# One attention-and-MLP kernel on one core: upper half-chains ten matmuls behind instead of fourteen, maxima eight steps ahead instead of seven, and transfers costed by kind in the order's planner

## The chip, the core and the metric

The kernel runs on one core of one Trainium2 chip. Its engines are TensorE (PE, with its weight loads shown apart as PEld), VectorE (DVE), ScalarE (ACT), GpSimd (POOL) and SyncE (SP), which here only issues transfers. The metric is the device time of one execution in microseconds (us).

## The reference, cut to what matters

Inputs are one sequence of 2048 rows of 512 numbers, four square weight matrices, two MLP weights of 512 x 1792 and 1792 x 512, and 32 gates, all float32.

```python
xn = layernorm(x)
q, k, v = xn @ wq, xn @ wk, xn @ wv            # 32 heads of 16, 4 segments of 512 rows
for s in range(4):
    logits = qs @ ks.T / 4 + mask              # mask adds -1e9 where key index > query index
    a_dot  = softmax(logits) @ vs
    a_mem  = phi(qs) @ M / (phi(qs) @ z + 1e-6)
    o      = g * a_mem + (1 - g) * a_dot
    M, z   = M + phi(ks).T @ vs, z + sum(phi(ks))
s = o @ wo
g = silu(relu(xn @ w1) @ w2)
out = x + s * g
```

`phi(t)` is `t + 1` for positive `t` and `exp(t)` otherwise. `M` and `z` are a memory carried from segment to segment.

## The kernel before, in words

The work is cut into four segments of 512 rows. A segment has four groups of eight heads, and a group (`n`, 0 to 15) two units of four heads (`u`, 0 to 31). For a unit the kernel computes the logits twice: once with queries on the partitions, only for the row maxima (`rowmax`, L1197 on PE, then the masked maximum L1203 on DVE), and once transposed (`expo`, L1249 on PE, then the exponential L1266 or L1260 on ACT). The maxima reach the second pass by a round trip: L1211 and L1212 on POOL, a transpose L1221 on DVE, a transfer to DRAM (L1223) and one back into a row of the stacked queries (L1224). `stack` (L1171) loads the queries and keys of a unit from DRAM into one of three slots. `pv` (L1295) multiplies the exponentials by the values.

Every large product is made of three matmuls for each float32 product (high part times high part, high times low, low times high). With a contraction of 128 rows it is split again into two halves of 64 rows, which lie in the lower and the upper half of the TensorE array and run side by side. A chain is all matmuls that add into one PSUM bank: twelve lower ones (L798) and twelve upper ones (L807), in the last part of the second MLP product six of each. By the code there are 176 such chains: 56 of the first MLP product, 64 of the second, 32 of the query and key projections, 12 of the value projection and 12 of the output projection. `lanes` writes them in pairs: each step gives PE one lower matmul and, taken from the queue `back`, one upper matmul of an earlier step. Upper and lower halves add into the same bank, so the first upper matmul of a chain waits on a semaphore, `turn`, which the last lower matmul of that chain increments (L801 to L807). A queue entry is taken when more than `BACK` entries lie in it, and a chain's first entry only when that chain's lower half has been written in full:

```python
if back and (len(back) > BACK or not m) and (not back[0][4] or back[0][1] in ended):
    high = back.popleft()
```

The order of all instructions on all engines is made before the kernel is built. Steps `t` run from -18 to 160; unit `v` has its five parts of `expo` in steps `5v` to `5v + 4`, and `rowmax` of unit `u` lies `LAG` steps earlier. Between these the chains are filled in. A planner (`Sched`) keeps a clock for each engine and one for the transfer rings, lets each engine take the pending operation with the earliest due time, and hands PE work by its own estimate of when operands are ready. `search` makes such an order several times, feeds back due times found backwards from what PE needed, and keeps the order with the earliest planned end. Nothing of the planner runs on the chip; only its order does.

Of the kernel before, what the change touches and what calls it, by code (L numbers as in the profile page):

```python
# [2 lines left out]

# [13 lines left out]
L = 512  # L17
D = 512
H = 32
# [17 lines left out]
FREE = 2  # L37
LAG = 7
BACK = 14
RESERVE = 20.48  # L40
# [3 lines left out]
PASSES = 12  # L44
FIRST = 3
FIT = 4
KEEP = False
SWITCH = 0.40
LOAD = 0.11
READ, WRITE = 1.0, 0.6  # L50
WARM = 1
# [31 lines left out]
class Sched:  # L83
# [175 lines left out]
def search(run, say=None):  # L259


    plan, total, ends, found = [], 560.0, {}, []
    for i in range(PASSES):
# [5 lines left out]
        if i < FIRST:  # L269
            continue  # L270
        e2 = ends
        for j in range(FIT):
            _, used, end, new, _ = run(plan, total, e2, taken)
            if say:
                say(i, j, end)
            assert [(str(a), b) for a, b in used] == [(str(a), b) for a, b in plan]
            found.append((end, plan, total, e2, taken))
            e2 = {k: 0.5 * v + 0.5 * e2.get(k, v) for k, v in new.items()}
        ends = min(found, key=lambda f: f[0])[3] if KEEP else e2
    return min(found, key=lambda f: f[0])  # L280


def emit(tc, PE, ACT, DVE, POOL, SP, cst, ps, dr, args, plan, left, ends, script=None):
# [155 lines left out]
    def planes():  # L439
        for nm, (t, k), c in (("q", DDR.next(), 0.0), ("k", DDR.next(), -1.0)):  # L440
            k = [f"{k}.{i}" for i in range(2)]
            pool(512, (), k, lambda t=t, c=c: POOL.memset(t, c), 0.0, 1e-3)
            for d, dk in SDR[nm].t:
                dma(k, [f"{dk}.c"], lambda d=d, t=t: SP.dma_start(d[:, 0, :], t), 2.0, 0.73, WRITE)

    def gates():
        dma((), ["bt"], lambda: SP.dma_start(bt, bass.AP(
            tensor=beta.tensor, offset=beta.offset, ap=[[0, 128], [1, H]])), 10.0, 0.1, 1.6)
        pool(10, (), ["pari"], lambda: POOL.iota(pari, pattern=[[0, 1]], base=0, channel_multiplier=1), 54.7)
# [30 lines left out]
    def load_one():  # L480
        nonlocal nload
        src, kn = plan[nload]
        raw, rk = IO.next(True)
        early = nload < 4
        dma((), [rk], lambda: SP.dma_start(raw.rearrange("p (k f) -> p k f", k=kn) if kn else raw, src),
            30.4 if early else 4.0, 0.93 if kn else 0.8)
        raws.append((raw, rk))
        nload += 1
# [103 lines left out]
    def lnload(s):  # L592
        LN[s] = xts = []
        for t in range(4):
            xt, k = IO.next(True)
            xts.append((xt, k))
            dma((), [k], lambda xt=xt, t=t: SP.dma_start(xt, x2[s * L + 128 * t:s * L + 128 * (t + 1), :]),
                7.2 if s == 0 else 8.0, 0.8)

# [281 lines left out]
    def silu(s, t):  # L881
# [9 lines left out]
        else:  # L891
            g, gk = gd[s]
            dma([k], [f"{gk}.{t}"], lambda: SP.dma_start(g[128 * t:128 * t + 128, :], sg), 18.7, 0.73, WRITE)
        if t == 3:
# [7 lines left out]
    def fetch(s, t):  # L902
# [5 lines left out]
        else:  # L908
            gt, gk = IO.next(True)
            g, k = gd[s]  # L910
            dma([f"{k}.{t}"], [gk], lambda: SP.dma_start(gt, g[128 * t:128 * t + 128, :]), 0.0, 0.85)
            xr, xk = IO.next(True)
        dma((), [xk], lambda: SP.dma_start(xr, x2[rows, :]), 11.2, 0.85)
        GX[s, t] = (gt, gk, xr, xk, rows)
# [21 lines left out]
    def output(s, t, po, pk, onpool):  # L936
# [6 lines left out]
        IO.held -= {gk, xk}  # L943
        dma([gk], [f"out{s}{t}"], lambda: SP.dma_start(out2[rows, :], gt), 10.1, 0.73, WRITE)

# [20 lines left out]
    def outhalf(s, t, i, po, pk):  # L966
# [10 lines left out]
        qu = ACT if i else SP  # L977
        dma([hk], [f"out{s}{t}{i}"], lambda: qu.dma_start(out2[rows, c], gt[:, c]), 0.0, 0.4, WRITE, "ACT" if i else "SP")

# [44 lines left out]
    def projout(n, nm, pp, pk, wk_):  # L1024
# [10 lines left out]
        twice, once = (d[:, 1::2, :], d[:, 2, :]) if nm == "q" else (d[:, 1:3, :], d[:, 3, :])  # L1035
        dma(hks, [f"{dk}.h"], lambda: SP.dma_start(twice, r32(th)[:, None, :].to_broadcast([128, 2, L])), 4.0, 1.4, WRITE)
        dma(lks, [f"{dk}.l"], lambda: SP.dma_start(once, r32(tl)), 4.0, 0.73, WRITE)
        if s > 0 if nm == "q" else s < NSEG - 1:
# [35 lines left out]
    def numden(n):  # L1074
# [21 lines left out]
        else:  # L1096
# [4 lines left out]
            for i, r in enumerate((0, 64)):  # L1101
                dma([f"{xk}.{i}"], [f"{k}e{r}"], lambda r=r: SP.dma_start(
                    t[0, r // 16:r // 16 + 4], ex[64 - r:128 - r:16]), 7.8, 0.1, WRITE)

    def swap(ex, xk):

        EE[15] = ee, ek = PHI["k"].t[0]
        for i, r in enumerate((0, 64)):
            dma([f"{xk}.{i}"], [f"{ek}{r}"], lambda r=r: SP.dma_start(ee[r:r + 64], ex[64 - r:128 - r]), 25.3, 0.5, WRITE)
        quotient()  # L1110
# [54 lines left out]
    def stack(n, q):  # L1165
# [3 lines left out]
        for nm, bank, b in (("q", QS, "Q"), ("k", KS, "K")):  # L1169
            d, dk = HL[n, nm]  # L1170
            dma([f"{dk}.{e}" for e in "chl"], [f"{b}{i0}"] + [f"Q{i0}m"] * (nm == "q"), lambda d=d, bank=bank: SP.dma_start(  # L1171
                r32(bank[i0]), d[64 * q:64 * q + 64].rearrange("(p r) i c -> (r i) p c", p=2)), 20.0, 1.55)

# [42 lines left out]
    def maxrows(u):  # L1216
# [5 lines left out]
        mx, xk = MXR.next()  # L1222
        dma([tk], [xk], lambda: SP.dma_start(mx, mT), 8.6, 0.1, WRITE)  # L1223
        dma([xk], [f"Q{u % NS}m"], lambda: SP.dma_start(  # L1224
            r32(QS[u % NS][0:128:32, :, :]).rearrange("r p (j b n) -> r (p j) b n", j=4, b=4),
            mx.rearrange("(b r j) n -> r j b n", b=4, r=4)), 24.6, 0.1)

# [51 lines left out]
    def pv(u, blocks):  # L1279
# [18 lines left out]
        if 2 in blocks:  # L1298
# [17 lines left out]
            for b in range(4):  # L1316
                two = late and b % 2
                dma(fk, [f"{nk}.{q}{b}"], lambda b=b, qu=ACT if two else SP: qu.dma_start(  # L1318
                    N_[64 * q + 16 * b:64 * q + 16 * b + 16, :], F[32 * b:32 * b + 16, :]),
                    (-5 if late else 3.7) + 0.2 * b, 0.11, WRITE, "ACT" if two else "SP")  # L1320
            if n < 15:
                d, k = DQ[n]
                dma(fk, [f"{k}d{q}"], lambda: SP.dma_start(d[1, 4 * q:4 * q + 4], F[16:128:32]), 14.6, 0.1, WRITE)
            else:
                dma(fk, [f"{dk}.{q}"], lambda: SP.dma_start(
                    D_[64 * q:64 * q + 64], F[16:128:32, None, :].to_broadcast([4, 16, L])), -5.1 if late else 3.7, 0.5, WRITE)
            if q == 1:
# [4 lines left out]
    def combine(n):  # L1332
# [18 lines left out]
        ks = [f"{k}d{q}" for q in range(2)] + ([f"{k}e{r}" for r in (0, 64)] if s else [])  # L1351
        dma(ks, [ck], lambda: SP.dma_start(c[:, i:], t[i:].rearrange("c h (s n) -> (h s) c n", n=32)), b + 0.7, 0.18)
        dve(0, [ck], [ck], lambda: DVE.reciprocal(c[:, i:], c[:, i:]), b + 8.9)
        S.pend["DVE"][-1].dur = 0.55 if s else 0.3
        dma([ck], [rk], lambda: SP.dma_start(r[i:].rearrange("c h (s n) -> (h s) c n", n=32), c[:, i:]), b + 11.8, 0.18, WRITE)
        dma([rk], dk, lambda: SP.dma_start(D_, r[1][:, None, :].to_broadcast([8, 16, L])), b + 2.0, 0.8)
        if DP:
# [3 lines left out]
        if s:  # L1361
            (E, ek), (G, gk) = EER.next(), NG.pop(n)
            ek = [f"{ek}.{q}" for q in range(2)]
            dma([rk], ek, lambda: SP.dma_start(E, r[0][:, None, :].to_broadcast([8, 16, L])), b + 14.7, 0.8)
        if s:
# [296 lines left out]
```

## Time and profile before

| | |
|---|---|
| median of 3 runs | 737.33 us (735.18 to 737.67) |
| the profiled execution | 738.45 us |
| its span, first to last instruction | 736.7 us, granted TensorE clock 0.996 |
| PE busy | 708.3 us, 96% of the span |
| DVE, ACT, POOL busy | 436.6, 412.9, 447.5 us |
| transfers | 139.88 MB, 59.1% of the 16 rings on the main queue |

Times in a timeline are microseconds from the span's start: start, duration, engine, line, operation and tiles. The recorded end of a matmul is modelled, and matmuls are pipelined, so the rate of PE is read from the distance between starts. L798 is a lower, L807 an upper half matmul.

### The profile page before, as it was taken

The page shows a single profiled execution, that of the slowest core. Times are in us where ns is not written, and L with a number is a line of the kernel's source. Part 1 is how long each engine was busy: PE and PEld are TensorE (multiplying, and loading weights), DVE is VectorE, ACT ScalarE, POOL GpSimd, SP SyncE. Part 2 cuts the span into 40 slices and gives each one's busy share as a digit, 9 for nine tenths or more (in the row PEclk, how much of TensorE's full clock was granted, in tenths as well). Part 3 has the DMA queues.
Part 4 walks back from the last instruction along what each step waited for, and adds up shares of the span by engine and source line. Part 5 has one row for each costly group of instructions (what it writes and reads, how often), then busy time and mean ns, then how long its engine had stood idle before and what let it go on. Part 6 is the DMA issues. An engine that isn't in the chain of part 4 may idle for free.

```text
span 736.7 us, 18668 instructions
## 1 busy us (share of the span) xinstructions
PE 708.3 (96%) x6834; PEld 554.0 (75%) x6834; DVE 436.6 (59%) x1397; ACT 412.9 (56%) x633; POOL 447.5 (61%) x568
## 2 busy tenths in 40 slices
PE   8999999999989999999998999999998998989997
PEld 7889777778766687786787768776766876667776
DVE  4157776678657564556675665564756356555527
ACT  5543647666656654555755674556565536554641
POOL 5543656547457666664775865677466646565674
PEclk9999999999999999999999999999999999999999
DMA  5777457467655576473756657647376756563423
GB/s 175 211 250 255 146 183 241 145 203 217 236 178 177 188 259 207 148 242 109 225 173 201 206 189 275 191 138 246 112 249 202 258 171 212 173 185 115 126 50 127
DMA packets 125491, 139.88 MB, mean 190 GB/s; under 512 B 24712, under 2 KB 70024, under 8 KB 125400
## 3 DMA queue, kind: packets, MB, share of 16 engines
q1 hardware_dynamic: 125192, 138.50, 59.1%
q8 instruction: 54, 0.88, 0.5%
q14 instruction: 37, 0.30, 0.1%
q10 hardware_dynamic: 208, 0.20, 0.1%
HBM read 99.01 MB, written 34.93 MB: 182 GB/s over the span
## 4 chain that ended last, share of the span: by engine, by line
PE 52%; DMA 22%; POOL 6%; DVE 6%; SPq 5%; issue 5%; ACT 3%; POOLq 0%; DVEq 0%; ACTq 0%
PE ps L798 29%; PE ps L807 7%; PE ps L1295 6%; PE pt L1249 4%; PE ps L1197 4%; DMA dd<-rq 3%; DMA rq<-cr 2%; DMA io<-in_B_w_dram 2%; DVE none L1203 2%; SPq L1318 2%; DMA io<-in_A_x_dram 2%; DMA out_dram<-io 2%; DMA io<-in_A_wq_dram 2%; POOL wl L497 2%; DMA ee<-rq 1%
## 5 line engine op out<-in xcount | busy, mean ns | idle before, releaser
L1203 DVE CUSTOM_DVE_ANT_0 none<-ps,causal 128x384 bf16<-128x384 f32 (+3 forms) x512 | 250.6, 489 | 113.7 <-PE ps L1197 81.5
L497 POOL TENSOR_TENSOR wl<-io,wh 128x512 fp32r<-128x512 f32 x176 | 226.4, 1296 | 117.7 <-ACT wh L496 97.4
L1266 ACT ACTIVATE P<-pt 128x1024 f32<-128x1024 f32 x128 | 131.0, 1023 | 48.6 <-PE pt L1249 41.7
L798 PE MATMUL ps<-xh,wh 64*128 64x512 f32 x352 | 140.5, 399 | 1.4 <-DVE md L1203 1.2
L807 PE MATMUL ps<-xl,wh 64*128 64x512 f32 x352 | 140.0, 398 | 0.0
L807 PE MATMUL ps<-xh,wl 64*128 64x512 f32 x352 | 137.6, 391 | 0.0
L807 PE MATMUL ps<-xh,wh 64*128 64x512 f32 x352 | 137.5, 391 | 0.0
L798 PE MATMUL ps<-xl,wh 64*128 64x512 f32 x352 | 137.3, 390 | 0.0
L798 PE MATMUL ps<-xh,wl 64*128 64x512 f32 x352 | 137.1, 390 | 0.0
L496 ACT ACTIVATE wh<-io 128x512 fp32r<-128x512 f32 x176 | 107.5, 628 | 48.8 <-DMA io<-in_B_w_dram 19.3
L1256 POOL TENSOR_SCALAR_AFFINE_SELECT P<-P 128x512 f32<-128x512 f32 x128 | 80.4, 638 | 67.0 <-ACT P L1266 55.0
L807 PE MATMUL ps<-wl,hh 64*128 64x512 f32 x224 | 90.2, 403 | 0.0
L798 PE MATMUL ps<-wh,hh 64*128 64x512 f32 x224 | 89.4, 399 | 0.4 <-DVE md L1203 0.4
L807 PE MATMUL ps<-wh,hl 64*128 64x512 f32 x224 | 87.3, 390 | 0.0
L807 PE MATMUL ps<-wh,hh 64*128 64x512 f32 x224 | 87.2, 389 | 0.0
L798 PE MATMUL ps<-wl,hh 64*128 64x512 f32 x224 | 87.0, 388 | 0.0
L798 PE MATMUL ps<-wh,hl 64*128 64x512 f32 x224 | 86.9, 388 | 0.0
L1249 PE MATMUL pt<-qs,ks 64*128 64x384 f32 (+3 forms) x512 | 70.2, 324 | 9.8 <-ACT P L1266 7.2
L1295 PE MATMUL ps<-P,vt 128*17 128x512 f32 (+3 forms) x1024 | 75.3, 434 | 1.3 <-DVE F L1033 1.3
L1197 PE MATMUL ps<-ks,qs 64*128 64x256 f32 (+3 forms) x512 | 72.9, 327 | 2.5 <-DVE md L1203 1.2
L798 PEld LDWEIGHTS ps<-xh,wh 64*128 64x128 f32 x352 | 65.3, 185 | 12.5 <-DVE md L1203 3.6
L798 PEld LDWEIGHTS ps<-xh,wl 64*128 64x128 f32 x352 | 65.1, 185 | 10.3
(173 smaller groups left out, 1718.7 us busy)
## 6 DMA issues: line engine op xcount, KB each, us to landing
io<-in_B_w_dram SPq DMA_DIRECT2D x112, 256.0 KB
qs<-sdq SPq DMA_DIRECT2D x32, 512.0 KB
ks<-sdk SPq DMA_DIRECT2D x32, 512.0 KB
sdq<-F SPq DMA_DIRECT2D x16, 512.0 KB
sdk<-F SPq DMA_DIRECT2D x16, 512.0 KB
io<-in_A_x_dram SPq DMA_DIRECT2D x28, 256.0 KB
io<-in_A_wv_dram SPq DMA_DIRECT2D x16, 256.0 KB
io<-in_A_wq_dram SPq DMA_DIRECT2D x16, 256.0 KB
```

The costliest lines, as they stand in the source:

```text
L496: act(512, [rk], [hk], lambda: ACT.activation(h, raw, AF.Copy), 7.0 + nsplit if early else 6.0)
L497: pool(512, [rk, hk], [lk], lambda: POOL.tensor_tensor(l, raw, r32(h), op=OP.subtract), 8.5 + 1.3 * nsplit if early else 25.4)
L798: i = PE.matmul(m[0], m[2][0][LO], m[2][1][LO], start=m[4], stop=False)
L807: PE.matmul(h[0], h[2][0][HI], h[2][1][HI], start=False, stop=h[5] is not None)
L1197: PE.matmul(two[a][0][:, o:o + w], qs[r, p, w - 128:w], ks[r, p, :w], start=True, stop=True)
L1203: dve(w + 40 + TTR, [pk, "causal"], [f"{dk}.{p}{a}{j}"], lambda p=p, j=j, o=o, w=w, a=a, pS=pS: DVE.tensor_tensor_reduce(none[:, :w], pS[: ...
L1249: PE.matmul(pT[:, a, o:o + w], ks[r, p, 128 * i:128 * i + 128], qs[r, p, 128 * i:], start=True, stop=True)
L1256: pool(512, ks, ks, lambda: POOL.affine_select(t, t, pattern=[[0, 4], [1, 128]], compare_op=OP.is_ge, fill=0.0, base=0, channel_multiplier ...
L1266: act(1024, tk, [both[p]], lambda: ACT.activation(P[:, 2 * p:2 * p + 2, :], pT, AF.Exp, scale=0.25), 18.5)
L1295: PE.matmul(pO[32 * b:32 * b + 17, 128 * i:], v, P[:, b, o:o + w], start=i == 0, stop=i == 3)
L1318: dma(fk, [f"{nk}.{q}{b}"], lambda b=b, qu=ACT if two else SP: qu.dma_start(N_[64 * q + 16 * b:64 * q + 16 * b + 16, :], F[32 * b:32 * b + ...
```

## The change

`LAG` goes from 7 to 8, so that each unit's maxima are computed one step earlier relative to its exponentials. `BACK` goes from 14 to 10. In the planner a transfer now has a kind, and each kind has three numbers, the time on the rings, the delay behind it and the delay when the rings are idle, with a term for queued work; before, each call had a cost of its own and one of two delays. An operation's earliest time starts at 0 and no longer at the moment of its recording. The search gets 30 further passes, each from one of the four best orders so far with due times moved at random by 0.5 us. What is computed, and every tile and transfer, stays.

```diff
-LAG = 7
-BACK = 14
+LAG = 8
+BACK = 10
...
-KEEP = False
+MORE = 30
+TOP = 4
+MOVE = 0.5
+SEED = 1
...
-READ, WRITE = 1.0, 0.6
+QUEUED = 0.4
+KINDS = {
+    "row": (0.84, 1.03, 2.43), "col": (1.06, 1.17, 2.51), "bc": (1.43, 1.47, 3.29), "stack": (1.60, 1.15, 3.16),
...
-        o.out, o.users, o.t = False, [], self.now
+        o.out, o.users, o.t = False, [], 0.0
...
         if o.cost is not None:
-            self.rings = max(self.rings, s + o.dur + 0.5) + o.cost
-            o.lat = self.rings + o.lat - s - o.dur
+            cost, tail, idle = o.cost
+            e = s + o.dur
+            queue = max(self.rings - e - 0.5, 0.0)
+            self.rings = max(self.rings, e + 0.5) + cost
+            o.lat = max(self.rings + tail - e, idle) + QUEUED * min(queue, 2.0)
...
+    rng = Random(SEED)
+    for i in range(PASSES, PASSES + MORE):
+        top = sorted({f[0]: f for f in found}.items())[:TOP]
+        _, plan, total, ends, _ = top[rng.randrange(len(top))][1]
+        ends = {k: v + rng.gauss(0.0, MOVE) for k, v in ends.items()}
+        spent, used, end, new, taken = run(plan, total, ends)
...
+        fit(i, used, taken, {k: 0.5 * v + 0.5 * ends.get(k, v) for k, v in new.items()}, spent, 2)
...
-    def dma(rd, wr, fn, dl, cost, lat=READ, eng="SP"):
+    def dma(rd, wr, fn, dl, kind, eng="SP"):
...
-        return S.op(eng, 0.6, rd, wr, fn, dl, lat, cost=cost)
+        return S.op(eng, 0.6, rd, wr, fn, dl, 0.0, cost=KINDS[kind])
```

The changed kernel is 24 lines longer ahead of the emitter: lower halves are L822 there, upper halves L831, the maxima's matmuls L1221 and the exponentials' L1273.

Apart from two warm-up transposes more at the start, PE has the same matmuls; their order moves nearly everywhere. Three places follow, each a piece of PE's order with the semaphores that a row waits for.

The first chain of the first MLP product at the start of the program, bank `ps_118`, before:

```order
L798 MATMUL ps_118<-xl_129,wh_103 128x512
L798 MATMUL ps_118<-xh_127,wl_110 128x512
L798 MATMUL ps_117<-xh_127,wh_104 128x512
L798 MATMUL ps_117<-xl_129,wh_104 128x512
L798 MATMUL ps_117<-xh_127,wl_111 128x512 [waits Pool_49]
L807 MATMUL ps_118<-xh_127,wh_103 128x512 [waits turn]
L798 MATMUL ps_117<-xh_127,wh_104 128x512
```

The same place in the change:

```order
L822 MATMUL ps_118<-xl_129,wh_103 128x512
L822 MATMUL ps_118<-xh_127,wl_110 128x512
L831 MATMUL ps_118<-xh_127,wh_103 128x512 [waits turn]
L822 MATMUL ps_117<-xh_127,wh_104 128x512 [waits Activation_49]
L831 MATMUL ps_118<-xl_129,wh_103 128x512
L822 MATMUL ps_117<-xl_129,wh_104 128x512
```

Three lower matmuls of the next chain stood between the last lower matmul of `ps_118` and the first upper one; now none does.

A later place, where chains follow each other (banks `ps_114`, `ps_115`, `ps_116`), before:

```order
L798 MATMUL ps_114<-xh_127,wl_106 128x512
L807 MATMUL ps_113<-xh_127,wh_105 128x512
L798 MATMUL ps_115<-xh_127,wh_100 128x512 [waits Activation_49]
L807 MATMUL ps_113<-xl_129,wh_105 128x512
L798 MATMUL ps_115<-xl_129,wh_100 128x512
L807 MATMUL ps_113<-xh_127,wl_112 128x512
L798 MATMUL ps_115<-xh_127,wl_107 128x512 [waits Pool_49]
L807 MATMUL ps_114<-xh_127,wh_99 128x512 [waits turn]
L798 MATMUL ps_115<-xh_127,wh_100 128x512
```

In the change:

```order
L822 MATMUL ps_115<-xl_129,wh_100 128x512
L831 MATMUL ps_114<-xh_127,wl_106 128x512
L822 MATMUL ps_115<-xh_127,wl_107 128x512
L831 MATMUL ps_115<-xh_127,wh_100 128x512 [waits turn]
L822 MATMUL ps_116<-xh_127,wh_101 128x512 [waits Activation_49]
L831 MATMUL ps_115<-xl_129,wh_100 128x512
```

Before, six other matmuls stood between the last lower and the first upper matmul of a bank; in the change the waiting upper matmul is the next instruction. Counted over the whole program, that is so for 160 of the 176 waits on `turn` in the change and for none before, where the least distance is three matmuls between. Runs of pairs that hold no other work number 212 in the change and 246 before, and take 2032 steps and 2044 steps.

The first maxima of a unit (`qs_82`, `ks_85`), among the parts of `expo` of an earlier one (`qs_80`, `ks_83`), before:

```order
L1249 MATMUL pt<-qs_80,ks_83 128x384 [waits Activation_49]
L1249 MATMUL pt<-qs_80,ks_83 128x384
L1249 MATMUL pt<-qs_80,ks_83 128x128 x2
L798 MATMUL ps_118<-xh_127,wh_104 128x512 [waits DVE_49]
L807 MATMUL ps_117<-xl_129,wh_102 128x512
L798 MATMUL ps_118<-xl_129,wh_104 128x512
L807 MATMUL ps_117<-xh_127,wl_109 128x512
L798 MATMUL ps_118<-xh_127,wl_111 128x512 [waits Pool_49]
L807 MATMUL ps_116<-xh_127,wh_103 128x512 [waits turn]
L1197 MATMUL ps_114<-ks_85,qs_82 128x512 [waits DMAHW2_49,DMAHW1_49,DVE_49]
L1197 MATMUL ps_115<-ks_85,qs_82 128x512 [waits DVE_49]
```

In the change, at a like place (unit in `qs_81`, `ks_84`):

```order
L1273 MATMUL pt<-qs_82,ks_85 128x512 [waits Activation_49]
L1273 MATMUL pt<-qs_82,ks_85 128x512
L1221 MATMUL ps_115<-ks_84,qs_81 128x512 [waits DMAHW4_49,DMAHW3_49]
L1221 MATMUL ps_118<-ks_84,qs_81 128x512 [waits DVE_49]
L822 MATMUL ps_113<-wh_101,hh_131 128x512
```

The first maxima of a unit, which wait for its two stack transfers, follow the third part of the earlier unit's `expo` before and its second part in the change.

More of the change, by code (lines that the diff above doesn't have):

```diff
@@ L2 @@
 from contextlib import ExitStack
+from random import Random
 import concourse.bass as bass
@@ L262, in search, with fit @@
     plan, total, ends, found = [], 560.0, {}, []
+    def fit(i, used, taken, e2, total, n):
+        for j in range(n):
+            _, got, end, new, _ = run(used, total, e2, taken)
+            if say:
+                say(i, j, end)
+            assert [(str(a), b) for a, b in got] == [(str(a), b) for a, b in used]
+            found.append((end, used, total, e2, taken))
+            e2 = {k: 0.5 * v + 0.5 * e2.get(k, v) for k, v in new.items()}
+        return e2
     for i in range(PASSES):
@@ L268, in search @@
         ends = {k: 0.7 * v + 0.3 * ends.get(k, v) for k, v in new.items()} if i else {}
[L269 to L279, printed above, removed]
+        if i >= FIRST:
+            ends = fit(i, used, taken, ends, total, FIT)
+    rng = Random(SEED)
[4 more added lines that the diff above has]
+        spent, used, end, new, taken = run(plan, total, ends)
+        if say:
+            say(i, -1, end)
+        fit(i, used, taken, {k: 0.5 * v + 0.5 * ends.get(k, v) for k, v in new.items()}, spent, 2)
     return min(found, key=lambda f: f[0])
@@ L443, in planes @@
             for d, dk in SDR[nm].t:
-                dma(k, [f"{dk}.c"], lambda d=d, t=t: SP.dma_start(d[:, 0, :], t), 2.0, 0.73, WRITE)
+                dma(k, [f"{dk}.c"], lambda d=d, t=t: SP.dma_start(d[:, 0, :], t), 2.0, "put")
     def gates():
         dma((), ["bt"], lambda: SP.dma_start(bt, bass.AP(
-            tensor=beta.tensor, offset=beta.offset, ap=[[0, 128], [1, H]])), 10.0, 0.1, 1.6)
+            tensor=beta.tensor, offset=beta.offset, ap=[[0, 128], [1, H]])), 10.0, "bt")
         pool(10, (), ["pari"], lambda: POOL.iota(pari, pattern=[[0, 1]], base=0, channel_multiplier=1), 54.7)
@@ L485, in load_one @@
         dma((), [rk], lambda: SP.dma_start(raw.rearrange("p (k f) -> p k f", k=kn) if kn else raw, src),
-            30.4 if early else 4.0, 0.93 if kn else 0.8)
+            30.4 if early else 4.0, "col" if kn else "row")
         raws.append((raw, rk))
@@ L597, in lnload @@
             dma((), [k], lambda xt=xt, t=t: SP.dma_start(xt, x2[s * L + 128 * t:s * L + 128 * (t + 1), :]),
-                7.2 if s == 0 else 8.0, 0.8)
+                7.2 if s == 0 else 8.0, "row")
     def stats(s, t, mv, mk, dl):
@@ L892, in silu @@
             g, gk = gd[s]
-            dma([k], [f"{gk}.{t}"], lambda: SP.dma_start(g[128 * t:128 * t + 128, :], sg), 18.7, 0.73, WRITE)
+            dma([k], [f"{gk}.{t}"], lambda: SP.dma_start(g[128 * t:128 * t + 128, :], sg), 18.7, "put")
         if t == 3:
@@ L910, in fetch @@
             g, k = gd[s]
-            dma([f"{k}.{t}"], [gk], lambda: SP.dma_start(gt, g[128 * t:128 * t + 128, :]), 0.0, 0.85)
+            dma([f"{k}.{t}"], [gk], lambda: SP.dma_start(gt, g[128 * t:128 * t + 128, :]), 0.0, "row")
             xr, xk = IO.next(True)
-        dma((), [xk], lambda: SP.dma_start(xr, x2[rows, :]), 11.2, 0.85)
+        dma((), [xk], lambda: SP.dma_start(xr, x2[rows, :]), 11.2, "row")
         GX[s, t] = (gt, gk, xr, xk, rows)
@@ L943, in output @@
         IO.held -= {gk, xk}
-        dma([gk], [f"out{s}{t}"], lambda: SP.dma_start(out2[rows, :], gt), 10.1, 0.73, WRITE)
+        dma([gk], [f"out{s}{t}"], lambda: SP.dma_start(out2[rows, :], gt), 10.1, "put")
     def wout(s):
@@ L977, in outhalf @@
         qu = ACT if i else SP
-        dma([hk], [f"out{s}{t}{i}"], lambda: qu.dma_start(out2[rows, c], gt[:, c]), 0.0, 0.4, WRITE, "ACT" if i else "SP")
+        dma([hk], [f"out{s}{t}{i}"], lambda: qu.dma_start(out2[rows, c], gt[:, c]), 0.0, "half", "ACT" if i else "SP")
     def wlast():
@@ L1035, in projout @@
         twice, once = (d[:, 1::2, :], d[:, 2, :]) if nm == "q" else (d[:, 1:3, :], d[:, 3, :])
-        dma(hks, [f"{dk}.h"], lambda: SP.dma_start(twice, r32(th)[:, None, :].to_broadcast([128, 2, L])), 4.0, 1.4, WRITE)
-        dma(lks, [f"{dk}.l"], lambda: SP.dma_start(once, r32(tl)), 4.0, 0.73, WRITE)
+        dma(hks, [f"{dk}.h"], lambda: SP.dma_start(twice, r32(th)[:, None, :].to_broadcast([128, 2, L])), 4.0, "put2")
+        dma(lks, [f"{dk}.l"], lambda: SP.dma_start(once, r32(tl)), 4.0, "put")
         if s > 0 if nm == "q" else s < NSEG - 1:
@@ L1102, in numden @@
                 dma([f"{xk}.{i}"], [f"{k}e{r}"], lambda r=r: SP.dma_start(
-                    t[0, r // 16:r // 16 + 4], ex[64 - r:128 - r:16]), 7.8, 0.1, WRITE)
+                    t[0, r // 16:r // 16 + 4], ex[64 - r:128 - r:16]), 7.8, "dq")
     def swap(ex, xk):
@@ L1108, in swap @@
         for i, r in enumerate((0, 64)):
-            dma([f"{xk}.{i}"], [f"{ek}{r}"], lambda r=r: SP.dma_start(ee[r:r + 64], ex[64 - r:128 - r]), 25.3, 0.5, WRITE)
+            dma([f"{xk}.{i}"], [f"{ek}{r}"], lambda r=r: SP.dma_start(ee[r:r + 64], ex[64 - r:128 - r]), 25.3, "half")
         quotient()
@@ L1171, in stack @@
             dma([f"{dk}.{e}" for e in "chl"], [f"{b}{i0}"] + [f"Q{i0}m"] * (nm == "q"), lambda d=d, bank=bank: SP.dma_start(
-                r32(bank[i0]), d[64 * q:64 * q + 64].rearrange("(p r) i c -> (r i) p c", p=2)), 20.0, 1.55)
+                r32(bank[i0]), d[64 * q:64 * q + 64].rearrange("(p r) i c -> (r i) p c", p=2)), 20.0, "stack")
     MR = {}
@@ L1222, in maxrows @@
         mx, xk = MXR.next()
-        dma([tk], [xk], lambda: SP.dma_start(mx, mT), 8.6, 0.1, WRITE)
+        dma([tk], [xk], lambda: SP.dma_start(mx, mT), 8.6, "mx")
         dma([xk], [f"Q{u % NS}m"], lambda: SP.dma_start(
             r32(QS[u % NS][0:128:32, :, :]).rearrange("r p (j b n) -> r (p j) b n", j=4, b=4),
-            mx.rearrange("(b r j) n -> r j b n", b=4, r=4)), 24.6, 0.1)
+            mx.rearrange("(b r j) n -> r j b n", b=4, r=4)), 24.6, "qm")
     PT, PO = {}, {}
@@ L1319, in pv @@
                     N_[64 * q + 16 * b:64 * q + 16 * b + 16, :], F[32 * b:32 * b + 16, :]),
-                    (-5 if late else 3.7) + 0.2 * b, 0.11, WRITE, "ACT" if two else "SP")
+                    (-5 if late else 3.7) + 0.2 * b, "nn", "ACT" if two else "SP")
             if n < 15:
                 d, k = DQ[n]
-                dma(fk, [f"{k}d{q}"], lambda: SP.dma_start(d[1, 4 * q:4 * q + 4], F[16:128:32]), 14.6, 0.1, WRITE)
+                dma(fk, [f"{k}d{q}"], lambda: SP.dma_start(d[1, 4 * q:4 * q + 4], F[16:128:32]), 14.6, "dq")
             else:
                 dma(fk, [f"{dk}.{q}"], lambda: SP.dma_start(
-                    D_[64 * q:64 * q + 64], F[16:128:32, None, :].to_broadcast([4, 16, L])), -5.1 if late else 3.7, 0.5, WRITE)
+                    D_[64 * q:64 * q + 64], F[16:128:32, None, :].to_broadcast([4, 16, L])), -5.1 if late else 3.7, "half")
             if q == 1:
@@ L1363, in combine @@
             ek = [f"{ek}.{q}" for q in range(2)]
-            dma([rk], ek, lambda: SP.dma_start(E, r[0][:, None, :].to_broadcast([8, 16, L])), b + 14.7, 0.8)
+            dma([rk], ek, lambda: SP.dma_start(E, r[0][:, None, :].to_broadcast([8, 16, L])), b + 14.7, "bc")
         if s:
```

6 lines of the change are left out of this document (3 added, 3 removed), and 3 rows, old and new, of the table KINDS.

## The prediction

> **What bounds the kernel now.** I read the page first: how busy each engine is, what clock was granted, and who is on the chain that ended last.
>
> ```profile
> PE 708.3 (96%) x6834; PEld 554.0 (75%) x6834; DVE 436.6 (59%) x1397; ACT 412.9 (56%) x633; POOL 447.5 (61%) x568
> PEclk9999999999999999999999999999999999999999
> PE 52%; DMA 22%; POOL 6%; DVE 6%; SPq 5%; issue 5%; ACT 3%; POOLq 0%; DVEq 0%; ACTq 0%
> ```
>
> PE is busy in 708.3 of 736.7 us, at a full clock throughout, and every other engine has a third of the span free. So PE's own stream sets the time, and the whole of what better timing of the others could win is what PE waits for them. The table of waits, for PE alone, tells how much that is:
>
> ```profile
> PE pt L1249 <- ACT P L1266: 7.2, 5, 2.9
> PE ps L1126 <- DVE mc L1162: 3.5, 2, 2.0
> PE pt L1249 <- DVE F L1093: 2.1, 4, 0.6
> PE pt L1084 <- ACT P L1266: 2.1, 2, 1.7
> PE ps L798 <- DVE md L1203: 1.6, 3, 1.0
> PE pt L565 <- POOL epst L364: 1.4, 1, 1.4
> PE ps L1295 <- DVE F L1033: 1.3, 1, 1.3
> PE ps L1197 <- DVE md L1203: 1.2, 2, 0.8
> ...
> PE pt L1249 <- DMA qs<-mx: 0.4, 1, 0.4
> ```
>
> The columns are total, times and longest. The eight largest add to 20.4 us; 1.4 us of that (L565) is the very start, which the change leaves alone. That leaves **19.0 us**, in few, long waits. The wait that an earlier start of the maxima addresses most directly, `expo` for the maxima's row (`qs<-mx`), is 0.4 us in all.
>
> Next comes the pace of PE. The timeline where one chain's upper half takes over, in the kernel before (L798 lower, L807 upper; the L798 at 29.02 is the last lower matmul of its chain, the L807 at 29.68 the first upper one, which waits on `turn`):
>
> ```profile
> 29.02 0.39 PE L798 MATMUL ps<-xh,wl 64*128 64x512 f32 x1
> 29.23 0.39 PE L807 MATMUL ps<-xl,wh 64*128 64x512 f32 x1
> 29.25 0.39 PE L798 MATMUL ps<-xh,wh 64*128 64x512 f32 x1
> 29.45 0.39 PE L807 MATMUL ps<-xh,wl 64*128 64x512 f32 x1
> ...
> 29.68 0.39 PE L807 MATMUL ps<-xh,wh 64*128 64x512 f32 x1
> 29.70 0.39 PE L798 MATMUL ps<-xh,wl 64*128 64x512 f32 x1
> ...
> 29.91 0.60 ACT L839 ACTIVATE hh<-ps 128x512 fp32r<-128x512 f32 x1 [3.67 <-PE ps L807]
> ```
>
> Each half starts a matmul every 0.23 us (29.23, 29.45, 29.68), and the two halves run side by side. The handover leaves no hole: from the last lower to the first upper matmul 0.66 us pass, and six other matmuls fill them. But a result takes longer than 0.23 us to be seen. ACT, idle for 3.67 us, starts 0.46 us after the start (29.45) of the matmul that it waited for.
>
> **Change, part one: BACK 14 to 10.** A chain of twelve cannot begin its upper half before its lower half is written, so with ten the queue is already over its length when the last lower matmul goes in, and the first upper one follows at once. In the order made by the change, 160 of 176 waits on `turn` stand directly behind the matmul that they wait for; before, three to six or more lay between. PE takes its matmuls in order, so behind that wait stand both halves of the array, and after PE the evacuations on ACT and DVE.
>
> What such a wait costs is not in the trace as it stands, but one place is near: the first chain, where three lower matmuls stood between and the upper half had nothing else to do.
>
> ```profile
> 26.30 0.39 PE L798 MATMUL ps<-xh,wl 64*128 64x512 f32 x1
> 26.53 0.39 PE L798 MATMUL ps<-xh,wh 64*128 64x512 f32 x1
> 26.76 0.39 PE L798 MATMUL ps<-xl,wh 64*128 64x512 f32 x1
> ...
> 26.81 0.18 PEld L807 LDWEIGHTS ps<-xh,wh 64*128 64x128 f32 x1
> 26.84 0.46 PE L807 MATMUL ps<-xh,wh 64*128 64x512 f32 x1
> ...
> 27.15 0.39 PE L807 MATMUL ps<-xl,wh 64*128 64x512 f32 x1
> ```
>
> The last lower matmul starts at 26.30, the weights of the first upper one load at 26.81 and it starts at 26.84: **0.54 us**. Directly behind, PE would have started the next pair after 0.23 us, so 0.31 us are lost. Then PE must also pick up again. The nearest row for that is a restart of both halves after another wait:
>
> ```profile
> 551.90 0.39 PE L798 MATMUL ps<-wh,hl 64*128 64x512 f32 x1
> 552.26 0.18 PEld L798 LDWEIGHTS ps<-xh,wh 64*128 64x128 f32 x1 [0.39 <-DVE hl L840]
> 552.26 0.50 PE L798 MATMUL ps<-xh,wh 64*128 64x512 f32 x1
> ...
> 552.60 0.40 PE L798 MATMUL ps<-xl,wh 64*128 64x512 f32 x1
> ...
> 552.84 0.39 PE L798 MATMUL ps<-xh,wl 64*128 64x512 f32 x1
> ```
>
> The first matmul after the hole takes 0.50 in place of 0.39 us, and the next starts 0.34 us behind it (552.26 to 552.60), 0.11 us more than the pace; from then on 0.24 and 0.23. So one wait costs 0.31 + 0.11 = **0.42 us**, and 160 cost **67 us**. Nothing hides it: the lost time is PE's own.
>
> Bounds for that price. Below: a reader can start 0.46 us after the matmul's start (ACT above), and if weights were ready by then and the restart cost nothing, 0.46 - 0.23 = 0.23 us, or 37 us in all. Above: 0.31 us and the whole excess of the restart, 552.26 to 552.84 being 0.58 in place of 0.46, gives 0.43, with rounding 0.45 us, or 72 us. I take 0.42, since the row at 26.84 is the very same wait.
>
> The Trainium skill speaks to the lower bound. Its page "TensorE: Matmul & The Clock Gate", section "Step-by-step: what each phase is for", says that PE pulls weight loads ahead of matmuls in flight when the row groups do not conflict; the upper half's weights would then be loaded while the wait lasts, and the sum would be the 37 us. The trace does not agree at this wait: the load stands at 26.81, 0.03 us before its matmul, though that half of the array had been free.
>
> The other side of part one: fewer steps without a partner. The changed order has 2032 steps for its pairs, 12 fewer, at 0.23 us each: **-3 us**. And results come out of a chain up to four steps earlier, 0.9 us, which the table of waits already bounds.
>
> **Part two: LAG 7 to 8.** A step is the distance between units over five: the first maxima matmul of unit 24 starts at 527.05, that of unit 0 at 47.0, so 20.0 us for a unit and 4.0 us for a step. What the extra step can win is the 0.4 us of `qs<-mx` and part of the waits on DVE. What it can cost is seen at the stacks, which can only be loaded when the last `expo` of their slot is done:
>
> ```profile
> 519.37 0.47 SPq L1171 DMA_DIRECT2D qs<-sdq  x1
> 527.05 0.44 PE L1197 MATMUL ps<-ks,qs 64*128 64x512 f32 x2
> L1197 PE MATMUL ps<-ks,qs x512: 215/383/503, 47.0 to 687.2; 64*128 64x128 f32 x44, 64*128 64x512 f32 x43, 64*128 64x256 f32 x43, 64*128 64x384 f32 x41
> 575.81 6.58 DMA qs<-sdq
> ```
>
> At this, the tightest of the 32 units, 7.7 us pass from issue to first use, and a stack took 6.58 us on the chain. Had the use come a step earlier and the issue not, 2.9 us would be short. Eight units, read in the same way, had less than the 10.6 us from issue to use that 6.58 and 4.0 make (7.7 to 9.7 us) and would be short by 12 us together. I take 0 for it: the planner places filling work ahead of maxima whose stack it expects late, and every unit's 20 us hold some five of the new waits, 2 us of slack for each transfer. Both ends stay: 0 and +12.
>
> **Part three: transfer kinds and the longer search.** No instruction is added on the chip; only the 19.0 us can go. With PE slower by nearly a tenth, ACT, DVE and the transfers gain slack against it, whichever order they have, so most of those waits go for that reason alone. I take two thirds, **-13 us**, with the ends 0 and -19.
>
> **Sum.** 738.45 (the profiled execution) + 67 - 3 - 13 = 789.5. The profiled execution is 1.1 us above the median of the runs shown (737.33), so **788** against that median. By the bounds: 737 + 37 - 3 - 19 = 752 below, 737 + 72 - 3 + 12 = 818 above, if every end fell together.
>
> **The rivals.**
>
> *The wait is free* (faster). The increment could arrive while the last lower matmul is still streaming, so that pairs go on at 0.23 us. Then only the gains remain: 737 - 3 - 13 = **721**. For it: the handover at 29.68 shows no hole. Against it: that one had 0.66 us of other work, and the row at 26.84 needs 0.54 us without it. This side decides when one wait costs less than (3 + 13)/160 = 0.10 us. Chance 0.06.
>
> *Half price.* Weights are in place when the wait ends and both halves resume at pace, 0.23 us for each: 737 + 37 - 3 - 13 = **758**. For it: ACT's 0.46 us. Against: the two rows that show a late weight load and a slow restart. This is also what the skill's page would give. Chance 0.14.
>
> *The stacks come late as well.* The 12 us of part two on top: **800**, up to 813 where the waits of the table stay. For it: 7.7 us against 6.58. Against: PE waits for no stack in the table, and the new holes give transfers time. Chance 0.12.
>
> *Swallowed.* The holes fall on times in which PE would have waited anyway. With 19 us of waits in some 20 places and 160 holes spread evenly, that cannot reach 67 us; chance 0.02, near 738.
>
> The forecast itself, one wait at 0.35 to 0.45 us and most old waits gone, holds 0.66 and lies in 774 to 802.
>
> **How the numbers follow.** The predicted time is 788. The forecast, the half price and the late stacks lie between 755 and 808, which leaves out about 0.15. A difference of 0.3%, 2.2 us, is about what runs of this kernel can tell from none; faster by more than that has the first rival's 0.06 less a little, 0.05; the same 0.02; slower the rest, 0.93.
>
> **What would show it.** In the changed profile each first upper matmul (L831) that waits on `turn` should start some 0.54 us after the L822 ahead of it, its weight load 0.03 us before it, and its second matmul 0.3 us on; each hole shows some 0.15 us idle (0.54 less the recorded 0.39), 24 us together, so PE's busy share should be near 95%, and the rest of the loss is stretched matmuls. ACT's and DVE's waits for PE should grow, and the waits of PE for ACT, DVE and POOL fall below 10 us. Weight loads 0.2 us ahead of those matmuls would speak for half price; L1221 waiting for `qs<-sdq` or `ks<-sdk` for the late stacks. The forecast is wrong if the distance over `turn` stays near 0.23 us, or if PE's other waits grow.

## The result

The changed kernel takes **785.11 us** (median of 4, 784.71 to 785.93) against 737.5 us before: a ratio of 1.064, 95% interval 1.059 to 1.069. The prediction was 788, range 755 to 808. The profiled execution's span is 783.7 us. Lines of its page follow: the busy times, the clock, the chain that ended last, and two groups (line, engine, operation, tiles and count, then busy us and mean ns, then the idle time before them and what ended it):

```profile
PE 752.2 (96%) x6838; PEld 570.9 (73%) x6838; DVE 444.5 (57%) x1397; ACT 415.2 (53%) x633; POOL 449.1 (57%) x568
PEclk9999999999999999999999999999999999999999
PE 96%; issue 3%; POOL 0%; DVE 0%; POOLq 0%; ACT 0%
PE ps L831 43%; PE ps L822 25%; PE ps L1319 9%; PE ps L1221 6%; PE pt L1273 5%; PE pt L1108 2%; PE pt L589 1%; PE ps L718 1%; PE ps L1150 1%; PE ps L780 1%; PE ps L782 1%; PE ps L781 1%; PE ps L1178 0%; POOL io L966 0%; PE pt L780 0%
L1227 DVE CUSTOM_DVE_ANT_0 none<-ps,causal 128x384 bf16<-128x384 f32 (+3 forms) x512 | 250.7, 490 | 171.9 <-PE ps L1221 145.3
L831 PEld LDWEIGHTS ps<-xh,wh 64*128 64x128 f32 x352 | 64.7, 184 | 51.3 <-issue 48.6
```

PE's busy share looks as it did, 96%, while PE is busy 44 us longer with the same matmuls (two warm-up transposes aside): most of the loss lies between the starts of matmuls whose records overlap, inside what the page counts as busy. The chain is PE nearly alone (52% before). The maxima on DVE now wait 145.3 us for PE (81.5 before). Before the loads of the upper weights `xh,wh` (L831) 51.3 us are idle, 48.6 of them with no engine named as the cause. The waits of PE are these; the columns are total us, times and longest, and the view counts only holes over 0.15 us:

```profile
PE ps L831 <- PE ps L822: 8.6, 53, 0.2
PE pt L589 <- POOL epst L388: 1.4, 1, 1.4
PE ps L822 <- DVE bacc L903: 0.3, 1, 0.3
PE ps L822 <- DVE md L1227: 0.2, 1, 0.2
```

A wait of PE for itself has come in, and the waits for the other engines are gone but for 1.9 us. One handover in the timeline, the first chain (last lower matmul at 26.38):

```profile
26.38 0.39 PE L822 MATMUL ps<-xh,wl 64*128 64x512 f32 x1
26.89 0.18 PEld L831 LDWEIGHTS ps<-xh,wh 64*128 64x128 f32 x1 [0.54 <-issue]
26.92 0.47 PE L831 MATMUL ps<-xh,wh 64*128 64x512 f32 x1
...
26.92 0.49 PE L822 MATMUL ps<-xh,wh 64*128 64x512 f32 x1
...
27.23 0.39 PE L831 MATMUL ps<-xl,wh 64*128 64x512 f32 x1
...
27.26 0.39 PE L822 MATMUL ps<-xl,wh 64*128 64x512 f32 x1
...
27.49 0.39 PE L822 MATMUL ps<-xh,wl 64*128 64x512 f32 x1
```

From 26.38 to 26.92 no matmul starts on either half, 0.54 us. The weights load only 0.03 us before the waiting matmul. The next starts follow 0.31 and 0.34 us later, then 0.23. From the last lower matmul (26.38) to the second lower one of the next chain (27.26) it is 0.88 us, where two steps at pace are 0.46: 0.42 us lost at this wait.

The other handovers of the trace are alike. At all 160 direct waits the first upper matmul starts 0.53 to 0.57 us after the last lower one (median 0.535), with its weight load 0.03 us ahead.

### The profile page after: what moved, and what is told of

It reads as the page before. It is cut to its first block, busy times and chain, and to the rows that moved or that the text cites. A ratio compares the mean times of both kernels' runs of the same rounds, so it can differ in the third digit from the quotient of the medians.

```text
span 783.7 us, 18674 instructions
## 1 busy us (share of the span) xinstructions
PE 752.2 (96%) x6838; PEld 570.9 (73%) x6838; DVE 444.5 (57%) x1397; ACT 415.2 (53%) x633; POOL 449.1 (57%) x568
## 4 chain that ended last, share of the span: by engine, by line
PE 96%; issue 3%; POOL 0%; DVE 0%; POOLq 0%; ACT 0%
PE ps L831 43%; PE ps L822 25%; PE ps L1319 9%; PE ps L1221 6%; PE pt L1273 5%; PE pt L1108 2%; PE pt L589 1%; PE ps L718 1%; PE ps L1150 1%; PE ps L780 1%; PE ps L782 1%; PE ps L781 1%; PE ps L1178 0%; POOL io L966 0%; PE pt L780 0%
## 5 line engine op out<-in xcount | busy, mean ns | idle before, releaser
L1227 DVE CUSTOM_DVE_ANT_0 none<-ps,causal 128x384 bf16<-128x384 f32 (+3 forms) x512 | 250.7, 490 | 171.9 <-PE ps L1221 145.3
L831 PE MATMUL ps<-xh,wh 64*128 64x512 f32 x352 | 143.7, 408 | 13.6 <-PE ps L822 4.9
L822 PE MATMUL ps<-xh,wh 64*128 64x512 f32 x352 | 144.5, 411 | 0.6 <-DVE bacc L903 0.3
L831 PE MATMUL ps<-xl,wh 64*128 64x512 f32 x352 | 139.3, 396 | 0.0
L822 PE MATMUL ps<-xl,wh 64*128 64x512 f32 x352 | 136.9, 389 | 0.0
L822 PE MATMUL ps<-xh,wl 64*128 64x512 f32 x352 | 136.8, 389 | 0.0
L831 PE MATMUL ps<-xh,wl 64*128 64x512 f32 x352 | 136.8, 389 | 0.0
L831 PEld LDWEIGHTS ps<-xh,wh 64*128 64x128 f32 x352 | 64.7, 184 | 51.3 <-issue 48.6
L831 PE MATMUL ps<-wh,hh 64*128 64x512 f32 x224 | 90.8, 406 | 7.3 <-PE ps L822 2.2
L822 PE MATMUL ps<-wh,hh 64*128 64x512 f32 x224 | 91.8, 410 | 0.0
L1221 PE MATMUL ps<-ks,qs 64*128 64x256 f32 (+3 forms) x512 | 89.8, 329 | 0.0
L1273 PE MATMUL pt<-qs,ks 64*128 64x384 f32 (+3 forms) x512 | 89.6, 326 | 0.0
L831 PE MATMUL ps<-wl,hh 64*128 64x512 f32 x224 | 89.2, 398 | 0.0
L822 PE MATMUL ps<-wl,hh 64*128 64x512 f32 x224 | 87.2, 389 | 0.0
L822 PE MATMUL ps<-wh,hl 64*128 64x512 f32 x224 | 87.1, 389 | 0.0
L831 PE MATMUL ps<-wh,hl 64*128 64x512 f32 x224 | 87.0, 388 | 0.0
L822 PEld LDWEIGHTS ps<-xh,wh 64*128 64x128 f32 x352 | 64.8, 184 | 9.3 <-issue 2.6
```

The lines of the kernel that those rows point to most:

```text
L822: i = PE.matmul(m[0], m[2][0][LO], m[2][1][LO], start=m[4], stop=False)
L831: PE.matmul(h[0], h[2][0][HI], h[2][1][HI], start=False, stop=h[5] is not None)
L1221: PE.matmul(two[a][0][:, o:o + w], qs[r, p, w - 128:w], ks[r, p, :w], start=True, stop=True)
L1227: dve(w + 40 + TTR, [pk, "causal"], [f"{dk}.{p}{a}{j}"], lambda p=p, j=j, o=o, w=w, a=a, pS=pS: DVE.tensor_tensor_reduce(none[:, :w], pS[: ...
L1273: PE.matmul(pT[:, a, o:o + w], ks[r, p, 128 * i:128 * i + 128], qs[r, p, 128 * i:], start=True, stop=True)
```

## The experiments

The theory: the cost is a latency of PE on itself, 0.54 us from a matmul's start to the start of one that waits for it, less what work stands between. The rival: the new order, its lag, costs or search, is worse. Each run's time is a median; ratios, with their 95% interval, are against the kernel before in the same set of runs, where its own median was 737.9 to 740.4 us.

**BACK back to 14 in the changed kernel.** As a rule three pairs then stand between the last lower and the first upper matmul.

```diff
-BACK = 10
+BACK = 14
```

> The changed kernel with BACK back at 14: the lag of eight, the transfer kinds and the longer search stay. No wait on turn then stands directly behind its matmul (least distance: three matmuls between). If the loss is the wait's (160 waits at 0.43 us = 69 us, less the 19 us of PE's other waits that hid under them), the time falls to 785 - 69 = 716 plus whatever of PE's waits for ACT and DVE comes back, 0 to 20 us: 716 to 738, most likely near 728. If the new order itself, with its lag, costs or search, were to blame, the time stays near 785.

Measured: **716.15 us**, ratio 0.973 (0.966 to 0.980). The order was not to blame: without the direct waits everything else in the change makes the kernel faster than before. The four longest of PE's waits there:

```profile
PE ps L1221 <- ACT F L1334: 1.5, 1, 1.5
PE pt L589 <- POOL epst L388: 1.4, 1, 1.4
PE ps L822 <- POOL ol L1393: 1.1, 1, 1.1
PE ps L822 <- DVE md L1227: 1.0, 2, 0.7
```

All of them add to 7.5 us, where the kernel before has 23. Few of them came back when PE's holes went, so the new order had removed most of them by itself. This run is faster than both kernels.

**BACK 13.**

```diff
-BACK = 10
+BACK = 13
```

> The changed kernel with BACK 13: the usual distance from the last lower to the first upper matmul is then four matmuls between, so the slot of the upper one lies 0.68 us behind (three steps at 0.23 us), later than the 0.54 us that the increment, the release and the weight load take. If the price is a latency of 0.54 us that later slots cover, this run equals that with 14 within some 5 us. If it were a price for each wait at any distance, it would stay near 785.

Measured: **720.80 us**, 0.981 (0.973 to 0.989). 4.6 us above 14, within what was expected. A distance of three steps, 0.68 us, covers the latency: in the trace the lower matmuls behind a handover keep their pace to within 0.01 us over six steps. So the 4.6 us are not the wait's; where they come from was not traced.

**BACK 10 in the kernel before.**

```diff
-BACK = 14
+BACK = 10
```

> The kernel before with BACK 10 alone: lag seven, the old costs and the short search stay. 160 of its waits on turn stand directly behind their matmul. If the wait is the cause: 737.5 + 69 - 3 - 19 = 785, within 6 us, and PE's other waits fall below 5 us. If the lag or the planner's new costs were the cause: 737.

Measured: **787.39 us**, 1.071 (1.064 to 1.079): the one number makes the whole loss. In its profile (span 789.2 us against 736.7) PE's wait for itself appears, and the others shrink from 23.2 to 4.8 us without the new kinds, lag and search:

```profile
PE ps L807 <- PE ps L798: 7.9, 48, 0.2
PE pt L1249 <- ACT P L1266: 2.3, 2, 2.0
PE pt L565 <- POOL epst L364: 1.4, 1, 1.4
PE pt L565 <- ACT xh L701: 0.7, 1, 0.7
PE ps L694 <- ACT io L625: 0.4, 1, 0.4
```

**The kernel before in its own order, with a direct wait added.** The first upper matmul of a chain also waits on the lower matmul just ahead of it, which belongs to the next chain. In the code a second semaphore, `near`:

```diff
+                    elif h and h[4]:
+                        i.then_inc(near, 1)
...
+                        if m and not m[5]:
+                            tc.declare_fence(PE.wait_ge(near, nears[0]).ins, group=f"near{nears[0]}")
```

> The kernel before with its order of instructions unchanged on every engine, and one wait more in 171 of the 176 handovers: the first upper matmul also waits on the lower matmul that stands directly ahead of it (of the next chain). Nothing else differs, so this is the price of a direct wait alone. If it is 0.43 us: 737.5 + 171 x 0.43 - 19 (PE's other waits, which go) = 792, within 8 us. By the half price (0.23 us): 737.5 + 39 - 19 = 758. If the order were to blame: 737.

Measured: **795.66 us**, 1.082 (1.075 to 1.089). Each engine has the same instructions in the same order as before; only the waits and their increments are added. A handover there, with the lower matmul that is waited for at 30.33:

```profile
30.33 0.38 PE L799 MATMUL ps<-xh,wl 64*128 64x512 f32 x1
...
30.83 0.18 PEld L815 LDWEIGHTS ps<-xh,wh 64*128 64x128 f32 x1 [0.54 <-issue]
30.86 0.47 PE L815 MATMUL ps<-xh,wh 64*128 64x512 f32 x1
```

0.53 us here, and a median of 0.54 over the trace, as in the changed kernel. The span grew by 57.2 us (736.7 to 793.9). PE's waits for other engines, its start included, fell from 23.2 to 4.3 us, so the added waits cost some 76 us, 0.44 us for each of 171.

**BACK 12, one pair between.**

```diff
-BACK = 10
+BACK = 12
```

> The changed kernel with BACK 12: at 107 of the handovers only one pair lies between the last lower and the first upper matmul, so the upper one's slot is 0.45 us behind, inside the 0.54 us by 0.09 us. If the price is what of 0.54 us the slots do not cover, plus up to 0.1 us for picking up again, each costs 0.09 to 0.19 us: 716 + 10 to 20 = 726 to 736. If the price falls only on a wait directly behind its matmul, the time equals that with 13 and 14: 714 to 722. If any wait shorter than today's costs the full 0.43 us: 760.

Measured: **742.41 us**, 1.006 (1.002 to 1.009): above the first two expectations (726 to 736, 714 to 722) and below the third (760). A handover there:

```profile
30.23 0.39 PE L822 MATMUL ps<-xh,wl 64*128 64x512 f32 x1
...
30.46 0.39 PE L822 MATMUL ps<-xh,wh 64*128 64x512 f32 x1
30.74 0.18 PEld L831 LDWEIGHTS ps<-xh,wh 64*128 64x128 f32 x1 [0.32 <-issue]
30.77 0.46 PE L831 MATMUL ps<-xh,wh 64*128 64x512 f32 x1
...
30.77 0.50 PE L822 MATMUL ps<-xl,wh 64*128 64x512 f32 x1
...
31.11 0.40 PE L822 MATMUL ps<-xh,wl 64*128 64x512 f32 x1
```

Again 0.54 us from the last lower matmul (30.23) to the first upper one, so the latency is the same and its uncovered part is 0.08 us. But picking up again is paid in full on both halves: 0.34 us to the next lower start. From 30.46 to 31.11 are 0.65 us for two steps of 0.23, 0.19 us lost; 107 of these make 20 us of the 26 by which the run lies above 14. That is the upper end of what I had allowed, which only holds if every wait pays the whole pick-up: a short hole costs almost as much pick-up as a long one. The other 6 us were not traced further; 13 and 14 differ by about as much.

So the time by the distance is 785 us (directly behind), 742 (one pair), 721 and 716 (two pairs and more). One latency of 0.54 us explains the two that lose and the two that do not. What remains is where the 21 us came from that the change gains with BACK 14.

**Transfer kinds alone, search alone, lag alone, kinds and lag.** Of the kernel before, with BACK 14 throughout: the planner's kinds (with the term for queued work and the earliest time of 0, which no run parted from them); the 30 further passes; `LAG = 8`; and the changed kernel with BACK 14 and `MORE = 0`.

> With 14 matmuls of lag, the changed planner left 716 us, some 21 us under the kernel before: so the rest of the change gains, and the gain is nearly all of PE's 19 us of waits. This run is the kernel before with the transfer kinds alone (lag of maxima seven, BACK 14, short search). If better transfer costs win it, the time is 717 to 724 and PE's waits fall below 10 us. If it is the longer search or the lag, 733 to 740.

> The kernel before with the longer search alone, on the old transfer costs, lag seven, BACK 14. A search can only pick what the planner believes; if the old costs are what misleads it, the time stays at 730 to 740. If many tries alone find an order with fewer waits, 717 to 724.

> The kernel before with LAG 8 alone. The wait that it addresses most directly is 0.4 us, so 732 to 742 if it is worth nothing by itself; if the tighter stacks cost, up to 750 with PE waiting on L1171's transfers; if the lag is what frees the maxima, 717 to 726.

> The changed kernel with BACK 14 and without the 30 further passes: lag eight and transfer kinds together, short search. If kinds and lag make the gain, 714 to 722, equal to the run with BACK 14 and the long search; if the long search makes it, 728 to 740.

Measured: kinds **732.66** us (0.994, 0.990 to 0.997), just under the 733 to 740 of the case that kinds alone do not win it; search **734.16** (0.996, 0.991 to 1.000), not told from no change; lag **742.33** (1.008, 1.003 to 1.012), slightly slower, and just above the 732 to 742 of "worth nothing by itself"; kinds and lag together **716.77** (0.973, 0.965 to 0.980), all of the gain without the longer search. With lag alone PE waits, among others, for what the early maxima need, the rival of the late stacks:

```profile
PE ps L1197 <- DMA ks<-sdk: 3.1, 2, 1.8
PE ps L1197 <- issue: 2.8, 2, 2.2
```

With kinds and the same lag PE waits for no stack. The traces agree with the reading that the kinds place the stacks earlier: with lag alone the later of a unit's two stack transfers is issued less than 6 us before the unit's first maxima in nine of 32 units, with kinds and lag in four. No run moved the stacks alone.

**Kinds and search without the lag, and a lag of nine.** The changed kernel with BACK 14 and `LAG` at 7 or 9.

> The changed kernel with BACK 14 and LAG 7: transfer kinds and long search without the earlier maxima. Kinds alone gave 733, lag alone 742, both 717. If the gain needs both, because the kinds let the planner place the stacks so that the earlier maxima find them loaded, this run stays at 728 to 736. If the long search can stand in for the lag, 715 to 722.

> The changed kernel with BACK 14 and LAG 9, one step of 4 us more. If earlier maxima go on helping, 708 to 714, since PE still waits some 6 us. If the stacks, which can only be loaded when the last exponentials of their slot are done, now set the time, PE waits for sdq or sdk and the time is 720 to 745.

Measured: seven **722.12** us (0.979, 0.971 to 0.987), nine **736.86** (0.996, 0.992 to 1.000). Seven missed both windows, but by 0.12 us only that of "the search can stand in for the lag": with the kinds, search takes 733 to 722, lag takes it to 717, both together to 716. Nine is past the edge, as expected: PE waits for the stacks again.

```profile
PE ps L1221 <- DMA qs<-sdq: 4.0, 4, 1.9
PE ps L1221 <- issue: 3.1, 1, 3.1
PE ps L1221 <- DMA ks<-sdk: 2.5, 2, 2.3
```

The profiles of all eight, with BACK 14 throughout, side by side (times are medians; the rest is of the profiled execution; the last column counts stretches of 3.4 us at half the granted clock, short of the last microseconds, and is taken up in the last section):

| run | time, us | PE's waits, us | PE busy, us | halved clock |
|---|---|---|---|---|
| before | 737.5 | 23.2 | 708.3 | 1 |
| search | 734.16 | 22.2 | 705.3 | 2 |
| lag eight | 742.33 | 24.5 | 711.7 | 4 |
| kinds | 732.66 | 11.3 | 715.7 | 4 |
| kinds, search | 722.12 | 10.2 | 708.4 | 2 |
| kinds, lag eight | 716.77 | 8.3 | 703.3 | 1 |
| kinds, lag eight, search | 716.15 | 7.5 | 701.4 | 0 |
| kinds, lag nine, search | 736.86 | 16.2 | 713.8 | 5 |

The waits halve in every run with kinds, but for the lag of nine, and in none without. So the kinds remove the waits, and kinds alone lose part of that again in longer busy time. That busy time goes down with the search or the lag of eight is measured; why is not shown. Lag and search without the kinds were not run.

## Why the prediction was right, and where it was off

*The mechanism and its price* held: 0.54 us from matmul to dependent matmul, weights loaded 0.03 us ahead, a slow second step. The forecast took 0.42 us a wait. The first handover shows 0.42; where six lower matmuls follow a wait without other work, the loss has grown to 0.44 at the sixth, since the pace comes back slowly; the run with added waits gives 0.44. The changed kernel against the same with BACK 14 gives 783.7 - 714.1 = 69.6 us of span, 0.44 for each of 160, and PE's waits for others are some 5 us less in it, which makes it 0.47 with them. The 67 us of the sum should have been 70 to 75.

*PE's other waits* were the mis-sized term. I took 13 of 19.0 us off; nearly all went, from 23.2 us with the start to 1.9 (1.4 of it the start). The 19.0 were the eight longest rows only; the shorter ones hold another 2.8 us. This error and that of the price go opposite ways: in spans, 736.7 - 3 - 21 and the measured 783.7 leave 71 us for the waits on `turn`, where the sum had 67, 3 and 13. That 788 came within 3 us is in part luck. The 3 us for steps without a partner were not tested by themselves. The reason that I gave, that a slower PE gives slack "whichever order they have", is shown by the two runs without the new planner (4.8 and 4.3 us left, from 23.2).

*Part three* was wrong in its worth, though not in this kernel's time. I argued that better planning could win only those waits. With BACK 14 the change wins 21 us. PE's waits fall from 23.2 to 7.5 us, which is 16 us of it, and busy time, which I had not put into the sum, by 7 (708.3 to 701.4). In the changed kernel this gain cannot be seen, because a PE that is nearly a tenth slower hides the same waits anyhow: with BACK 10 the old planner's order takes 787.39 and the new one's 785.11. The two edits do not add.

*Part two*, nothing for the lag: not contradicted inside this change, where kinds, lag and search together are worth 2 us at BACK 10 (787.39 to 785.11); no run took out the lag alone there. In the kernel before the lag alone costs 4 us, less than the 12 I had bounded it by, and with the kinds it gains 16 (732.66 to 716.77). The 4 us are not simply the stacks': PE's waits add to only 1.3 us more than before, its busy time to 3.4 more. My reading of the stacks had also looked at the queries' transfer alone. The keys' transfer leaves less, 3.7 us in unit 0 and 7.1 in unit 26, where I called 7.7 the tightest.

*The rivals.* The free wait (721) and the half price (758) fell with the run of added waits and with the weight loads, 0.03 us ahead at all 160 waits. The Trainium skill's page "TensorE: Matmul & The Clock Gate", section "Step-by-step: what each phase is for", from which the half price followed, has PE pull weight loads ahead of matmuls in flight when the row groups do not conflict; across these waits the trace shows none pulled ahead. The late stacks are real, but only for the lag alone and for nine.

Of the signs named, the 24 us of idle holes came true, though the table of waits shows 8.6: that table leaves out holes of 0.15 us and less, which most of these are. The idle time before the first upper matmuls is in the groups by line:

```profile
L831 PE MATMUL ps<-xh,wh 64*128 64x512 f32 x352 | 143.7, 408 | 13.6 <-PE ps L822 4.9
L831 PE MATMUL ps<-wh,hh 64*128 64x512 f32 x224 | 90.8, 406 | 7.3 <-PE ps L822 2.2
L831 PE MATMUL ps<-wh,oh 64*128 64x512 f32 x48 | 19.6, 408 | 1.8 <-PE ps L822 0.9
L831 PE MATMUL ps<-wh,xh 64*128 64x512 f32 x48 | 19.5, 407 | 1.8 <-PE ps L822 0.5
```

Together they are 24.5 us, 0.15 for each wait. They took the place of the old waits, so the idle total hardly moved and the busy share stayed at 96%, where I wrote 95. The remaining 0.27 us or more of each wait is the 44 us of longer busy time. The distance of starts was the better sign.

## What to carry to other kernels

When two streams share an engine and one waits on the other through a semaphore, count the instructions between producer and waiter, and keep more work there than one instruction's full latency (here 0.54 us, three steps of 0.23 us), since here the wait stopped both. A planner that has no term for this cannot warn of it: its order with BACK 10 is 69 us worse than with 14. And a gain in an engine's waits for others must be judged with that engine at full pace, because here a slower PE hid the same waits.

## What was not expected of the hardware

The granted clock of PE can halve without a long wait. In the run with kinds alone, windows of the timeline show this (start and end, length, PE busy us and matmuls, granted clock, share and GB/s of transfers):

```profile
567.40:570.80 3.40, 3.40 (x25) 1.00 0.20 41
570.80:574.20 3.40, 2.62 (x15) 0.99 0.55 165
574.20:577.60 3.40, 3.30 (x14) 0.50 0.76 238
577.60:581.00 3.40, 3.40 (x15) 0.50 0.69 204
581.00:584.40 3.40, 3.40 (x18) 0.50 0.93 328
584.40:588.00 3.60, 3.60 (x46) 1.00 0.08 30
```

Before the clock fell PE waited at most 0.62 us at once, and mostly one half of the array worked. Then the clock was 0.50 for three stretches of 3.4 us; in the first two PE was busy nearly all the while, for the greater part with one half. Where one half works alone, a matmul then starts every 0.43 us in place of 0.23. In the other halved stretches of the runs here a hole of some 1 to 3.3 us came just before. The kernel before has one, after its longest wait:

```profile
615.40:618.80 3.40, 1.38 (x16) 1.00 0.71 228
618.80:622.20 3.40, 3.40 (x24) 0.50 0.88 263
```

Short of the last microseconds, the changed kernel has no such stretch, and neither has it with BACK 14, 13 or 12 and its lag of eight; the counts of the other runs are in the table above, and the kernel before with BACK 10 has one. A wait of PE, or a while with half of the array, can so cost more than its own length. As an estimate from the 0.43 and 0.23 us, one stretch costs at most 1.6 us, so the three that kinds alone has more than kinds and lag are at most 5 of the 16 us between them, and the three that lag alone has more than the kernel before could be its 4 us. That the waits and the half-used array bring the halving is read from what came before it; no run took the halved clock away by itself.
